# A new hand-written order for the first chunk of a fused attention and feed-forward kernel

## The chip, the cores and the metric

The kernel runs on one core of a Trainium2 chip. The metric is the device time of one execution in microseconds (us); lower is better. All times of the trace are counted from the first instruction of the profiled execution. PE stands for TensorE, DVE for VectorE, ACT for ScalarE, POOL for GpSimd, SP for SyncE.

## What is computed

Eight batches of eight heads with 576 positions and 64 features each go through masked attention. Heads 0 to 3 see the last 32 positions ("local"), heads 4 to 7 the positions with the same remainder modulo 32 ("strided"). The result, 4608 rows of 512, goes through two matrices with a softplus between them.

```
scores = where(mask, (q @ k.T) / 8, -1e9)            # 8 x 8 heads, 576 x 576
attn   = softmax(scores) @ v                         # 576 x 64 a head
x      = attn, heads side by side                    # 4608 x 512
h      = x @ w_in                                    # 512 -> 2048
g      = maximum(h, 0) + log1p(exp(-abs(h)))
out    = g @ w_out                                   # 2048 -> 512
```

## The kernel before, in words

Heads are worked in pairs: four pairs a batch, 32 in all (n = 0 to 31). The feed-forward part goes over nine chunks of 512 rows, and in each chunk over sixteen slices f of 128 hidden features. Each of x, g and the weights is split into a high and a low part, and three matmuls of 512 columns (high*high, twice, and low*high) stand for one product. So a chunk and slice takes 12 matmuls for `hidden` (L648, x to h) and 12 for `output` (L688, g to the result). The weights come as 64-bit floats and are turned into two 32-bit parts on the chip, once, in the first chunk; later chunks use the parts that lie in SBUF.

The first chunk therefore carries four kinds of work at once: the attention of pairs 0 to 3 (without which no feed-forward matmul can start), the attention of pairs 4 to 7, the conversion of 32 weight tiles, and the feed-forward of chunk 0 and the first two slices of chunk 1. Its order is written out by hand: `FIRST` (L36) is one string of task names, and at L946 a loop calls each task once, in this order. Every engine and every DMA queue works through its own instructions in the order in which the tasks issued them, waiting where a semaphore says so. From the third slice of chunk 1 on, a planner (`Plan`, with costs and due times) makes the order; the change does not touch it.

Three more lists, `ON_POOL`, `ON_VECTOR` and `ON_SCALAR`, say which engine does a task that several can do; a task in none of them goes to its usual engine.

The names: a letter or two, then the pair n or the slice f, and for pairs a part or half.

| name | what it does | engine (usual) |
|---|---|---|
| `q4`, `k4`, `v4` | DMA of pair 4's q, k, v, on SP's queue | SP (L261, L282, L293/L300) |
| `wi4`, `wo4` | DMA of slice 4's tile of w_in, w_out, 512 KB | SP (L569, L575) |
| `D4` (`D00`, `D01` a head) | q laid out for the score matmuls | ACT (L264) |
| `S40`, `S41` | score matmuls, part 0 and 1 | PE (L340, L355) |
| `X`, `x`, `E` | maximum of each row, its negative, exponentials | DVE (L389), DVE/POOL (L393), ACT (L399) |
| `Y`, `E`, `Z` | the same for the parts 00, 11, 20, 30 in wide form | DVE, ACT (L381), DVE (L385) |
| `r`, `R`, `M` | sum plus 1e-9, reciprocal, multiplication | DVE (L439), DVE, POOL or DVE (L447) |
| `T`, `C` (n < 4) | transposes by matmul and their copies out of PSUM | PE, ACT or DVE (L264) |
| `P` (n > 3) | 16 transposes on VectorE | DVE (L457) |
| `V40`, `V41` | weighted sums with v, by halves | PE (L525) |
| `H`, `L` | high and low part of x out of PSUM | ACT (L563), DVE (L561) |
| `ai`, `Bi`, `di`, `ci` (`ao`...) | four steps of the conversion of a w_in (w_out) tile | ACT (L589), DVE (L593, L602, L619) |
| `hi`, `li` (`ho`, `lo`) | high and low 32-bit part of the tile | ACT or POOL (L264), POOL or DVE (L634) |
| `F4`, `O4` | `hidden` and `output` of slice 4 (`Fa` the first three pairs of x alone) | PE (L648, L688) |
| `A`, `Ae`, `Al`, `u` | abs, exp, log, then the softplus sum | ACT three times, DVE (L669) |
| `Gh`, `Gl` | high and low part of g | ACT or DVE or POOL, POOL or DVE (L681) |
| `Qa`, `Q`, ... | the same steps for slices 0 and 1 of chunk 1 | |
| `y0` to `y3` | results of chunk 0 to DRAM | ACT or DVE, then SP (L704) |

Buffers that order work: one PSUM bank for scores of pairs 4 and up (`ps`), one for the sums with v (`pv`), two for `hidden` (`ph`), two buffers for u, three each for the parts of g, four for the conversion. K of pair n lies in one of two tiles, `kT`, so `k8` may be loaded when `S61` has read pair 6's. Pair 4's q lands where pair 3's probabilities were.

```
        for name in names:
            first[name]()
        plan.run()
```

Of the kernel before, what the change touches and what calls it, by code (L numbers as in the profile page):

```python
# [33 lines left out]


FIRST = """  # L36
q0 D00 k0 W mask D01 S01 q1 X01 x01 D11 q2 D10 S00 X00 Y00 E01 D20 E00 Z00 r0 D21 R0 M0 k1 S10 X10
S11 wi2 ai2 X11 Y11 E11 T00 wi4 k2 S20 ai4 Bi2 x10 E10 di2 k3 ci2 Bi4 Z11 hi2 di4 r1 ci4 T01 C01
C00 q3 D30 D31 T02 X20 R1 Y20 M1 v0 V00 C02 H00 wi1 E20 ai1 S21 X21 L00 Z20 T10 wi0 li2 x21 T11
hi4 Bi1 di1 ci1 E21 r2 V01 H01 L01 C11 wo0 S31 C10 R2 v1 hi1 S30 X30 wo14 li4 wo1 T12 Y30 ai0 X31  # L40
M2 V10 H10 L10 T21 k4 C12 Bi0 v2 wi3 x31 E30 di0 Z30 V11 C21 E31 H11 T20 C20 li1 L11 ao1 T22 r3 R3
M3 V20 T32 ao0 ci0 C22 Bo0 H20 L20 C32 hi0 ai3 T30 C30 do0 wo3 li0 T31 V21 v3 co0 C31 V31 H21 L21
ho0 V30 Bi3 di3 ao3 H30 Fa0 Bo3 ci3 hi3 H31 L30 wi10 q4 D4 L31 F0 lo0 A0 Fa1 do3 co3 li3 Ae0 ho3
Al0 Bo1 do1 u0 S40 X40 wo4 ao4 lo3 Bo4 wo2 ao2 x40 Bo2 Gh0 Gl0 wi8 ai8 wo9 wi6 Bi8 E40 F1 F3 A3
Ae3 do2 di8 ci8 hi8 Al3 co2 do4 co1 ho1 wo5 A1 Ae1 Al1 u3 li8 Gh3 O0 lo1 ho2 lo2 ai6 u1 wi5 ai5
S41 wi11 X41 x41 Gl3 Bi5 Gh1 Gl1 ai11 Bi11 Bi6 E41 F4 wo7 q5 D5 wi9 wi15 F2 A2 di5 O1 di11 Ae2 Al2
di6 ci5 r4 hi5 ci6 wi14 R4 wi12 ci11 hi11 k5 wi13 u2 Gh2 M4 S50 X50 F8 co4 x50 P4 Gl2 O2 li11 A4
Ae4 hi6 ho4 li5 li6 Al4 u4 E50 S51 X51 v4 V40 ai9 Bi9 di9 x51 A8 wo6 Ae8 Al8 wi7 k6 q6 lo4 wo11
ao5 Bo5 O3 ci9 ai7 Bi7 di7 u8 Gh4 Gl4 F5 H40 L40 E51 ci7 ai10 Bi10 r5 R5 F6 Gh8 do5 D6 S60 hi7
di10 Gl8 co5 M5 V41 ci10 A5 Ae5 Al5 u5 O4 li7 A6 Ae6 Al6 X60 x60 u6 ho5 P5 Gh5 Gl5 hi9 lo5 wo12  # L50
li9 F7 H41 hi10 ao7 li10 v5 O5 ao6 Bo6 do6 L41 co6 E60 S61 X61 Gh6 Gl6 A7 Ae7 Al7 x61 Bo7 k7 V50
u7 F9 ho6 lo6 O6 wo10 H50 L50 ai13 Bi13 wo8 ao8 E61 q7 V51 Bo8 D7 di13 do7 A9 Ae9 ci13 r6 R6 hi13
S70 do8 li13 F13 co8 H51 co7 M6 Al9 u9 Gh7 ao10 X70 x70 L51 ho8 Gl7 F10 P6 ho7 ai12 lo7 Gh9 Gl9
lo8 E70 Bi12 Bo10 O7 ao9 Bo9 do10 S71 v6 V60 do9 k9 O8 co9 ho9 A13 Ae13 Al13 u13 F11 di12 A10 Ae10
Al10 Gh13 X71 u10 ao11 Bo11 co10 ho10 lo9 lo10 Gh10 Gl10 x71 H60 L60 do11 ai14 Bi14 O9 A11 V61
ci12 di14 E71 r7 R7 O10 hi12 ai15 ci14 Ae11 li12 H61 L61 co11 hi14 M7 li14 wo15 Al11 u11 F12 P7
Gh11 Gl11 wo13 ao12 A12 Ae12 F14 ho11 lo11 Gl13 ao13 Al12 u12 Gh12 A14 Ae14 Bo12 do12 Gl12 co12
ho12 O11 Bi15 di15 lo12 ci15 ao15 Bo15 v7 V70 H70 L70 ao14 Bo14 Qa0 Al14 u14 O12 q8 D8 hi15 li15
Bo13 do13 co13 ho13 lo13 do14 co14 ho14 V71 H71 F15 A15 Ae15 L71 O13 Q0 Gh14 Gl14 lo14 O14 Al15
u15 Gh15 Gl15 Q1 v8 do15 co15 ho15 lo15 QA0 Qu0 QA1 O15 y0 Qh0 k8 Ob15 Ql0 y3 y2 Qu1 Qh1 Ql1 y1 q9  # L60
"""
# [958 lines left out]
```

## Time and profile before

| what | us |
|---|---|
| median of 3 runs (lowest 898.74, highest 899.64) | 899.62 |
| the profiled execution's own time | 898.62 |
| span of its instructions | 896.8 |
| PE busy | 878.9 |
| DVE busy | 601.3 |
| ACT busy | 446.8 |
| POOL busy | 58.1 |

The profile is one execution. Busy time is the time in which at least one instruction of the engine was running. A row of the timeline reads: start, duration, engine, line, operation, tile written<-tiles read, shapes, how many, and in brackets how long the engine sat idle before it and whose end released it. A row of the windows gives busy time and number of instructions of each engine in a stretch; a row of the waits gives total, number and longest. Matmuls overlap their successors, so their starts tell more than their durations.

### The profile page before, as it was taken

How to read it: one execution, taken by the hardware profiler on the slowest of the kernel's cores; microseconds unless marked ns; L12 is line 12 of the kernel's file. 1: busy time of each engine (PE TensorE's matmuls, PEld its weight loads, DVE VectorE, ACT ScalarE, POOL GpSimd, SP SyncE). 2: the span in 40 equal slices, each digit the busy share in tenths (PEclk: the TensorE clock that was granted, in tenths of full speed). 3: DMA queues.
4: the chain of work that ended last, by engine and by line, in shares of the span. 5: the costliest groups of instructions: out<-in, count | busy, mean ns of one | idle time of the engine just before them, and what ended most of it. 6: DMA issues, size and time to landing. Idle time of an engine off the chain costs nothing.

```text
span 896.8 us, 14347 instructions
## 1 busy us (share of the span) xinstructions
PE 878.9 (98%) x5632; PEld 722.0 (81%) x5632; DVE 601.3 (67%) x1313; ACT 446.8 (50%) x795; POOL 58.1 (6%) x81
## 2 busy tenths in 40 slices
PE   6899999999999999999999999999999999999998
PEld 4777777888888888888888888888888888888886
DVE  8999996877777677666766676776776333333332
ACT  7998765445444545544544444454443343333332
POOL 6244330000000000000000000000000000000000
PEclk9999999999999999999999999999999999999999
DMA  9882212112211112111211121111200010001001
...
DMA packets 50083, 58.27 MB, mean 65 GB/s; under 512 B 3168, under 2 KB 35296, under 8 KB 50016
## 3 DMA queue, kind: packets, MB, share of 16 engines
...
q8 instruction: 44, 0.72, 0.3%
q10 hardware_dynamic: 288, 0.33, 0.1%
...
## 4 chain that ended last, share of the span: by engine, by line
PE 87%; DVE 8%; ACT 2%; issue 1%; POOL 1%; DMA 0%; SPq 0%; DVEq 0%; POOLq 0%; ACTq 0%
PE py L688 41%; PE ph L648 40%; PE ps L355 2%; PE pv L525 2%; DVE pt L457 2%; PE po L525 1%; PE po L355 1%; DVE a_i L602 1%; DVE a_i L619 1%; DVE a_i L593 1%; DVE u L669 1%; DVE a_o L602 1%; DVE st L389 1%; DVE a_o L619 0%; DMA kT<-in_qk_dram 0%
## 5 line engine op out<-in xcount | busy, mean ns | idle before, releaser
L688 PE MATMUL py<-w_o,gh 128*128 128x512 f32 x1152 | 359.2, 393 | 0.3 <-POOL w_o L634 0.2
L648 PE MATMUL ph<-x_h,w_i 128*128 128x512 f32 x1152 | 356.4, 391 | 1.3 <-DVE w_i L634 0.9
L660 ACT ACTIVATE u<-ph 128x512 f32<-128x512 f32 x144 | 86.2, 599 | 396.8 <-PE ph L648 394.7
L648 PEld LDWEIGHTS ph<-x_h,w_i 128*128 128x128 f32 x1152 | 215.6, 188 | 47.2 <-DVE w_i L634 1.2
L688 PEld LDWEIGHTS py<-w_o,gh 128*128 128x128 f32 x1152 | 214.1, 188 | 47.7 <-POOL w_o L634 1.1
L648 PE MATMUL ph<-x_l,w_i 128*128 128x512 f32 x576 | 224.4, 390 | 0.0
L688 PE MATMUL py<-w_o,gl 128*128 128x512 f32 x576 | 224.4, 390 | 0.0
L669 DVE SCALAR_TENSOR_TENSOR u<-ph,u 128x512 f32<-128x512 f32 x144 | 99.2, 689 | 169.5 <-ACT u L665 167.9
L457 DVE STREAM_TRANSPOSE pt<-prob 32x192 f32<-32x192 f32 x448 | 137.1, 314 | 6.4
L688 PEld LDWEIGHTS py<-w_o,gl 128*128 128x128 f32 x576 | 108.2, 188 | 22.6
L648 PEld LDWEIGHTS ph<-x_l,w_i 128*128 128x128 f32 x576 | 108.2, 188 | 22.5
L681 DVE TENSOR_TENSOR gl<-u,gh 128x512 fp32r<-128x512 f32 x137 | 94.8, 692 | 12.0 <-POOL gh L264 0.8
L663 ACT ACTIVATE u<-u 128x512 f32<-128x512 f32 x144 | 91.2, 633 | 4.5
L665 ACT ACTIVATE u<-u 128x512 f32<-128x512 f32 x144 | 91.0, 632 | 4.3
L264 ACT COPY qT<-prob 64x576 f32<-64x576 f32 x56 | 70.6, 1261 | 2.3 <-DMA prob<-in_qk_dram 1.9
L264 DVE CAST gh<-u 128x512 fp32r<-128x512 f32 x130 | 55.7, 428 | 10.6 <-DVE u L669 0.5
L416 DVE TENSOR_TENSOR prob<-ps,mask_b 128x384 f32<-128x384 f32 x24 | 13.4, 558 | 50.2 <-PE ps L355 50.2
L355 PEld LDWEIGHTS ps<-kT,qT 128*64 128x64 f32 x720 | 24.0, 138 | 9.6 <-issue 8.1
L355 PE MATMUL ps<-kT,qT 128*64 128x64 f32 x720 | 27.6, 225 | 0.9 <-DMA kT<-in_qk_dram 0.9
L525 PE MATMUL pv<-pt,v_in 128*64 128x96 f32 x396 | 22.1, 248 | 1.0 <-PE ps L355 1.0
L447 DVE TENSOR_TENSOR prob<-prob,st 128x576 f32<-128x576 f32 x27 | 21.6, 799 | 0.9
L416 DVE TENSOR_TENSOR prob<-po,mask_b 128x192 f32<-128x192 f32 x24 | 8.6, 357 | 19.3 <-ACT x_h L563 19.3
(101 smaller groups left out, 511.9 us busy)
## 6 DMA issues: line engine op xcount, KB each, us to landing
...
```

Of the source, the lines that this page charges most:

```text
L264: (engine.copy if engine is nc.scalar else engine.tensor_copy)(dst, src)
L355: nc.tensor.matmul(ps[rows[place], 64 * (x - lo) : 64 * (x - lo) + 64], lhsT=blocks_of(n)[:, c // 32].rearrange("p h l -> p (h l)"), rhs=k ...
L416: nc.vector.tensor_tensor(pv, sv, m, op=ALU.add)
L457: nc.vector.transpose(pt[32 * (i + c) : 32 * (i + c) + 32, h, a : a + hi - lo, 32 * i : 32 * i + 32,], src[:, lo:hi, 32 * c : 32 * c + 32],)
L525: nc.tensor.matmul(po[64 * h : 64 * h + 64, TILE * x : TILE * x + TILE], lhsT=vs[n][:, a, h, :], rhs=pt_of(n, a)[:, h, a % 2], start=True, ...
L648: nc.tensor.matmul(ph, lhsT=w32["i", f][:, half, cc * P : (cc + 1) * P], rhs=x_of(x, cc)[:, t0 : t0 + n], start=(i == 0), stop=(i == 3 * N ...
L660: nc.scalar.activation(us[c, f], phs[c, f], AF.Abs)
L663: nc.scalar.activation(u, u, AF.Exp, scale=-1.0)
L665: nc.scalar.activation(u, u, AF.Ln, bias=1.0)
L669: nc.vector.scalar_tensor_tensor(u, in0=phs.pop((c, f)), scalar=0.0, in1=u, op0=ALU.max, op1=ALU.add)
L681: engine.tensor_tensor(g, us.pop((c, f)), ghs[c, f].bitcast(F32), op=ALU.subtract)
L688: nc.tensor.matmul(py[t], lhsT=g[:, sl], rhs=w32["o", f][:, half], start=(f == 0 and n == 0), stop=(f == NFC - 1 and n == 2),)
```

## The change

Only the tables change: the string `FIRST` holds the same names in another order, and the lists of engines hold other names. No function, no buffer and no planner cost changes. The first two lines of the order and the lists, in full:

```diff
 FIRST = """
-q0 D00 k0 W mask D01 S01 q1 X01 x01 D11 q2 D10 S00 X00 Y00 E01 D20 E00 Z00 r0 D21 R0 M0 k1 S10 X10
-S11 wi2 ai2 X11 Y11 E11 T00 wi4 k2 S20 ai4 Bi2 x10 E10 di2 k3 ci2 Bi4 Z11 hi2 di4 r1 ci4 T01 C01
...
+W mask q0 D00 k0 D01 S00 X00 Y00 q1 D11 S01 X01 E00 x01 Z00 k1 D10 S11 X11 q2 D20 Y11 E01 r0 wi0
+S10 X10 D21 x10 k2 S21 ai0 wo0 q3 D31 S20 R0 M0 E10 Bi0 di0 ci0 X21 hi0 E11 T00 x21 C00 ao0 Z11 r1
...
 ON_POOL = """
-x01 D10 D20 hi2 D30 hi0 hi3 ho1 x50 hi6 Gh8 x60 hi13 x70 ho9 Gh13 x71 ho11 hi15 ho14 Gh15 ho15
+D10 D20 x10 D31 hi0 x21 r2 x31 r3 hi3 hi1 ho1 Gh0 ho2 x41 hi4 r4 x50 x51 x60 Gh6 x61 r6 ho8 ho10
+ho9 x71 r7 hi14 hi15 ho13 ho14 ho15
 ON_VECTOR = """
-D00 M1 C21 M3 li0 lo0 li3 Gl0 li8 Gh3 lo1 Gl3 Gl1 lo4 Gl8 M5 Gl6 li13 lo9 lo10 Gl10 li12 M7 Gl12
-lo12 li15 lo13 Gh14 Gl14 lo14 Gl15 lo15
+D01 M0 C00 M3 li3 li1 li2 lo1 Gl0 li9 lo2 li4 Gl1 Gl4 li6 lo6 Gl6 lo7 Gl7 li12 lo8 M6 Gl9 lo11
+li14 M7 lo13 Gl14 Gl15
 ON_SCALAR = """
-y3
+y1 y3
```

The list for POOL has one line more, so every later line number is higher by one in the changed kernel. What this does to the instructions is shown at three places, as the built programs hold them.

VectorE, from the multiplication of pair 3 (`M3`) to the low part of pair 2's second half (`L21`). A name like `a_i_0` is the conversion buffer of w_in's tile 0, `a_o_0` of w_out's, `x_l1<-pv_2_0` the low part of x from pair 2, half 0. Before:

```order
L447 TENSOR_TENSOR prob_103<-prob_103,st_3_425 128x9x64
L619 SCALAR_TENSOR_TENSOR a_i_0_444<-ri_0_361,a_i_0_444 128x512
L593 TENSOR_SCALAR a_o_0_541<-a_o_0_541 128x512
L561 TENSOR_TENSOR x_l1_548<-pv_2_0_523,x_h1_546 128x288
L602 SCALAR_TENSOR_TENSOR a_o_0_541<-ro_0_395,a_o_0_541 128x512
L634 TENSOR_TENSOR w_i_0_551<-a_i_0_444,w_i_0_551 128x512
L619 SCALAR_TENSOR_TENSOR a_o_0_541<-ro_0_395,a_o_0_541 128x512
L561 TENSOR_TENSOR x_l1_548<-pv_2_1_582,x_h1_546 128x288
```

The same place on VectorE in the changed kernel:

```order
L448 TENSOR_TENSOR prob_103<-prob_103,st_3_353 128x9x64
L620 SCALAR_TENSOR_TENSOR a_i_1_386<-ri_1_368,a_i_1_386 128x512
L594 TENSOR_SCALAR a_i_2_512<-a_i_2_512 128x512
L562 TENSOR_TENSOR x_l1_525<-pv_2_0_515,x_h1_523 128x288
L603 SCALAR_TENSOR_TENSOR a_i_2_512<-ri_2_510,a_i_2_512 128x512
L635 TENSOR_TENSOR w_i_3_528<-a_i_3_396,w_i_3_528 128x512
L635 TENSOR_TENSOR w_i_1_576<-a_i_1_386,w_i_1_576 128x512
L562 TENSOR_TENSOR x_l1_525<-pv_2_1_579,x_h1_523 128x288
```

The tiles of slice 0 are converted earlier now, and tiles 1, 2 and 3 of w_in stand here instead.

ScalarE around the laying out of pair 6's q (`D6`, the two copies to `qT`), from the high parts of g's slice 4 and of pair 4's x on. `w_i_7<-a_i_7` is `hi7`, the activation from `ps_5_1` is `E51`. Before:

```order
L264 CAST gh_0_4_1016<-u_0_4_941 128x512
L563 CAST x_h0_331<-pv_4_0_970 128x288
L399 ACTIVATE prob_103,st_5_893<-ps_5_1_958,st_5_893 128x64 x3
L589 ACTIVATE a_i_10_1039<-ri_10_634 128x512
L264 COPY qT_99<-prob_103 64x18x32
L264 COPY qT_99<-prob_103 64x32x18
L264 CAST w_i_7_1077<-a_i_7_1011 128x512
L660 ACTIVATE u_0_5_1092<-ph_0_5_1020 128x512
```

The same place on ScalarE in the changed kernel:

```order
L564 CAST x_h0_325<-pv_4_0_971 128x288
L265 CAST gh_0_4_981<-u_0_4_936 128x512
L400 ACTIVATE prob_103,st_5_856<-ps_5_1_951,st_5_856 128x64 x3
L265 CAST w_i_7_1002<-a_i_7_849 128x512
L590 ACTIVATE a_o_4_1006<-ro_4_897 128x512
L265 COPY qT_99<-prob_103 64x18x32
L265 COPY qT_99<-prob_103 64x32x18
L661 ACTIVATE u_0_8_1024<-ph_0_8_989 128x512
```

`hi7` stood behind `D6` and stands ahead of it now, and `E51`, `D6` come after the first steps of slice 5 instead of before them.

SP's queue near the load of pair 8's k (`k8`, the DMA into `kT_0`). `prob` is a load of q (`q8` before, `q7` after). Before, with `v8` ahead and the results `y0` to `y2` (`out_0_dram`) around it:

```order
L261 DMA prob_103<-in_qk_dram 128x576
L293 DMA v_in_102<-in_v_dram 96x128
L300 DMA v_in_102<-in_v_dram 128x5x128
L704 DMA out_0_dram<-o_0_0_1778 128x512
L282 DMA kT_0_100<-in_qk_dram 128x576
L704 DMA out_0_dram<-o_0_3_1792 128x512
L704 DMA out_0_dram<-o_0_2_1795 128x512
```

SP's queue near the same load in the changed kernel, where `v5` stands ahead:

```order
L294 DMA v_in_102<-in_v_dram 96x128
L301 DMA v_in_102<-in_v_dram 128x5x128
L262 DMA prob_103<-in_qk_dram 128x576
L576 DMA ro_9_1228<-in_moe_w_out_dram 128x512
L283 DMA kT_1_101<-in_qk_dram 128x576
L283 DMA kT_0_100<-in_qk_dram 128x576
L570 DMA ri_13_1322<-in_moe_w_in_dram 128x4x128
```

`k8` left its place behind the first result and follows `k7` now.

On TensorE the score matmuls `S41`, `S50`, `S60` and `S70` each have one block of 12 feed-forward matmuls less ahead of them than before, and `S71` has three more.

More of the change, by code (lines that the diff above doesn't have):

```diff
@@ L36 @@
 FIRST = """
-q0 D00 k0 W mask D01 S01 q1 X01 x01 D11 q2 D10 S00 X00 Y00 E01 D20 E00 Z00 r0 D21 R0 M0 k1 S10 X10
-S11 wi2 ai2 X11 Y11 E11 T00 wi4 k2 S20 ai4 Bi2 x10 E10 di2 k3 ci2 Bi4 Z11 hi2 di4 r1 ci4 T01 C01
-C00 q3 D30 D31 T02 X20 R1 Y20 M1 v0 V00 C02 H00 wi1 E20 ai1 S21 X21 L00 Z20 T10 wi0 li2 x21 T11
-hi4 Bi1 di1 ci1 E21 r2 V01 H01 L01 C11 wo0 S31 C10 R2 v1 hi1 S30 X30 wo14 li4 wo1 T12 Y30 ai0 X31
-M2 V10 H10 L10 T21 k4 C12 Bi0 v2 wi3 x31 E30 di0 Z30 V11 C21 E31 H11 T20 C20 li1 L11 ao1 T22 r3 R3
@@ L42 @@
[L42 to L59, printed above, removed]
@@ L60 @@
-u15 Gh15 Gl15 Q1 v8 do15 co15 ho15 lo15 QA0 Qu0 QA1 O15 y0 Qh0 k8 Ob15 Ql0 y3 y2 Qu1 Qh1 Ql1 y1 q9
+W mask q0 D00 k0 D01 S00 X00 Y00 q1 D11 S01 X01 E00 x01 Z00 k1 D10 S11 X11 q2 D20 Y11 E01 r0 wi0
+S10 X10 D21 x10 k2 S21 ai0 wo0 q3 D31 S20 R0 M0 E10 Bi0 di0 ci0 X21 hi0 E11 T00 x21 C00 ao0 Z11 r1
+X20 T01 C01 Bo0 D30 v0 R1 do0 V00 H00 T02 C02 L00 Y20 co0 M1 k3 S31 X31 E21 E20 Z20 V01 li0 wi1
+S30 H01 L01 ai1 Bi1 r2 di1 x31 R2 M2 wi3 ai3 T10 C10 T11 C11 v1 T12 ho0 lo0 Bi3 V10 T21 X30 Y30
+di3 C12 H10 L10 V11 E30 T20 E31 Z30 C21 ci3 H11 v2 L11 r3 R3 M3 C20 ci1 T22 wi2 ai2 Bi2 V20 C22
@@ new lines @@
+H20 L20 di2 hi3 li3 T32 k4 wo1 C32 wi9 T31 ao1 T30 C31 v3 C30 hi1 li1 V21 H21 wo2 ao2 L21 V31 wi4
+V30 ci2 Bo1 Bo2 ai9 H31 L31 Fa0 q4 H30 L30 F0 wi10 do1 co1 Bi9 di9 wo3 Fa1 hi2 li2 D4 S40 ci9 A0
+Ae0 Al0 ho1 lo1 ao3 F1 u0 Gh0 X40 x40 F2 Bo3 Gl0 ai4 Bi4 hi9 li9 di4 do2 co2 ho2 v4 A1 ci4 E40 S41
+X41 x41 wi5 ai5 q5 Bi5 Ae1 Al1 u1 wo15 D5 lo2 O0 wi6 hi4 di5 li4 F3 Gh1 Gl1 O1 ci5 A2 Ae2 wi8 ai8
+do3 co3 ai10 k5 E41 S50 r4 hi5 wo12 Bi8 li5 Al2 A3 di8 u2 R4 Ae3 M4 Al3 wi7 ai7 ci8 wi12 hi8 X50
+x50 F4 u3 Gh3 Bi10 di10 ci10 F5 Gh2 Gl2 wo5 wo4 ho3 lo3 E50 P4 O2 A4 Gl3 q6 hi10 ao5 Bo5 Ae4 Al4
@@ new lines @@
+u4 wi11 S51 A5 Ae5 li8 X51 li10 ai6 Al5 Bi7 di7 V40 ci7 H40 x51 Gh4 Gl4 E51 r5 F8 hi7 do5 u5 ao4
+L40 O3 D6 Bi6 A8 Ae8 Al8 wi14 V41 H41 Bo4 li7 di6 do4 co4 ho4 ci6 hi6 R5 M5 k6 wo6 lo4 co5 Gh5 S60
+u8 Gh8 X60 F7 ao6 ho5 x60 E60 Gl5 li6 F6 A6 O4 ai11 L41 P5 wo7 ao7 wo8 Gl8 A7 Bo6 do6 Bo7 Ae6 Al6
+v5 V50 H50 S61 Ae7 Al7 lo5 O5 co6 ho6 u6 Gh6 Bi11 L50 do7 X61 x61 ai12 Bi12 F9 lo6 q7 wo9 D7 Gl6
+V51 co7 di12 E61 di11 ci11 H51 L51 ho7 k7 S70 X70 ci12 u7 lo7 hi11 li11 r6 k8 A9 O6 ao9 Bo9 x70
+Gh7 Ae9 Gl7 ao8 F11 do9 Bo8 do8 co8 Al9 u9 wi13 ai13 Bi13 di13 hi12 li12 wi15 ho8 lo8 co9 wo10
@@ new lines @@
+ao10 Bo10 O7 R6 ci13 M6 A11 do10 hi13 F10 O8 co10 ho10 Ae11 Al11 Gh9 u11 Gh11 ho9 lo9 F12 Gl9 O9
+lo10 P6 wo11 A10 Ae10 Al10 u10 ao11 Bo11 ao12 E70 S71 ai15 do11 Bi15 v6 V60 q8 Gl11 A12 Ae12 co11
+li13 F13 Gh10 H60 X71 L60 ai14 Bo12 V61 k9 Gl10 wo14 di15 H61 Al12 do12 L61 u12 Bi14 co12 O10 wo13
+ho11 lo11 di14 ci14 ci15 A13 Ae13 Al13 u13 Qa0 x71 E71 r7 hi14 R7 O11 li14 Gh13 F14 ho12 lo12 Gh12
+Gl12 O12 Gl13 A14 Ae14 Al14 M7 P7 u14 hi15 li15 ao13 Bo13 ao14 do13 co13 ao15 v7 V70 ho13 H70 F15
+A15 L70 V71 H71 lo13 Bo14 do14 co14 ho14 lo14 O13 Ae15 L71 v8 Al15 u15 Gh15 Q1 Gh14 Gl14 O14 Bo15
@@ L61 @@
+do15 D8 Q0 QA1 co15 Gl15 Qu1 QA0 Qu0 ho15 lo15 O15 Qh0 y0 Ob15 q9 y1 Qh1 Ql0 y2 y3 Ql1
 """
 ON_POOL = """
-x01 D10 D20 hi2 D30 hi0 hi3 ho1 x50 hi6 Gh8 x60 hi13 x70 ho9 Gh13 x71 ho11 hi15 ho14 Gh15 ho15
+D10 D20 x10 D31 hi0 x21 r2 x31 r3 hi3 hi1 ho1 Gh0 ho2 x41 hi4 r4 x50 x51 x60 Gh6 x61 r6 ho8 ho10
+ho9 x71 r7 hi14 hi15 ho13 ho14 ho15
 """.split()
 ON_VECTOR = """
-D00 M1 C21 M3 li0 lo0 li3 Gl0 li8 Gh3 lo1 Gl3 Gl1 lo4 Gl8 M5 Gl6 li13 lo9 lo10 Gl10 li12 M7 Gl12
-lo12 li15 lo13 Gh14 Gl14 lo14 Gl15 lo15
+D01 M0 C00 M3 li3 li1 li2 lo1 Gl0 li9 lo2 li4 Gl1 Gl4 li6 lo6 Gl6 lo7 Gl7 li12 lo8 M6 Gl9 lo11
```

## The prediction, made before the changed kernel was run

> **What bounds the kernel now.** I read the page first: the span and the busy rows of the engines.
>
> ```profile
> span 896.8 us, 14347 instructions
> PE 878.9 (98%) x5632; PEld 722.0 (81%) x5632; DVE 601.3 (67%) x1313; ACT 446.8 (50%) x795; POOL 58.1 (6%) x81
> ```
>
> TensorE is busy for 878.9 of 896.8 us, so it sat idle for 17.9 us in all. The change neither adds nor removes a matmul; it can win or lose only in that idle time. Where the idle time lies is told by the windows: the attention before the first feed-forward matmul, the rest of the first chunk, the seam to the planner's part, and a stretch behind it.
>
> ```profile
> 0.00:33.00 33.00, 22.40 (x482) 17.34 (x483) 28.60 (x61) 25.85 (x69) 18.40 (x42) 1.00 0.88 306
> 33.00:143.00 110.00, 107.47 (x666) 84.99 (x665) 104.84 (x222) 88.14 (x201) 39.67 (x39) 1.00 0.42 144
> 143.00:150.00 7.00, 6.06 (x57) 4.81 (x57) 4.14 (x8) 3.35 (x6) 0.00 (x0) 1.00 0.83 276
> 300.00:400.00 100.00, 100.00 (x640) 82.86 (x639) 71.30 (x164) 47.79 (x73) 0.00 (x0) 1.00 0.17 50
> ```
>
> The first figure behind the comma is PE, then its weight loads, DVE, ACT, POOL, the clock, the DMA share. TensorE idles for 10.6 us up to 33, for 2.5 us from 33 to 143, for 0.94 us at the seam, and not at all from 300 to 400, where the planner's order is untouched. VectorE is the second full engine: 104.84 of the 110 us of the first chunk. So both are near their limit there, and a kernel that idled nowhere after 33 us would be only 3.5 us shorter. The waits of TensorE between 33 and 150 us name the places:
>
> ```profile
> PE pv L525 <- PE ps L355: 1.0, 1, 1.0
> PE ps L355 <- DMA kT<-in_qk_dram: 0.9, 1, 0.9
> PE ph L648 <- DVE w_i L634: 0.9, 1, 0.9
> PE ph L648 <- DVE u L669: 0.3, 1, 0.3
> PE py L688 <- POOL w_o L634: 0.2, 1, 0.2
> ```
>
> Then I looked at how the feed-forward starts, in the timeline of TensorE, VectorE and ScalarE around 32 us:
>
> ```profile
> 32.00 0.72 PE L525 MATMUL pv<-early_l,room 128*64 128x96 f32 x12 [0.16 <-DVE x_l L561]
> 32.64 0.73 PE L648 MATMUL ph<-x_h,w_i 128*128 128x512 f32 x2
> 31.05 0.40 ACT L563 CAST x_h<-pv 128x288 fp32r<-128x288 f32 x1
> 31.50 0.45 DVE L561 TENSOR_TENSOR x_l<-pv,x_h 128x288 fp32r<-128x288 f32 x1
> 25.39 0.31 ACT L399 ACTIVATE prob<-py,st 128x64 f32<-128x64 f32 x1 [0.94 <-DVE st L393]
> ```
>
> The first feed-forward matmul, `Fa0`, begins at 32.64, behind `V30`, which waited for the one PSUM bank of the sums until `L21` had emptied it (31.50 to 31.95). `L21` began 0.05 us behind the end of `H21` on ScalarE (31.45). So VectorE and ScalarE reach this point together, and both must get earlier for `Fa0` to get earlier. The last row is the one long wait of ScalarE on that way: `E31` waited 0.94 us for `x31` on VectorE.
>
> **Part 1, the start.** The durations of the steps come from the rows by line (minimum, median and maximum in ns):
>
> ```profile
> L593 DVE TENSOR_SCALAR a_i<-a_i x16: 411/420/1512, 11.0 to 123.0; 128x512 uint32<-128x512 uint32 x16
> L602 DVE SCALAR_TENSOR_TENSOR a_i<-ri,a_i x16: 681/692/1784, 11.6 to 123.4; 128x512 uint32<-128x512 uint32 x16
> L619 DVE SCALAR_TENSOR_TENSOR a_i<-ri,a_i x16: 631/686/1783, 12.3 to 124.7; 128x512 uint32<-128x512 uint32 x16
> L634 DVE TENSOR_TENSOR w_i<-a_i,w_i x6: 673/686/1635, 30.3 to 127.0; 128x512 fp32r<-128x512 f32 x6
> L393 DVE TENSOR_SCALAR st<-st x7: 152/163/1270, 11.5 to 84.0; 128x3 f32<-128x3 f32 x5, 128x6 f32<-128x6 f32 x2
> L439 DVE TENSOR_SCALAR st<-st x32: 157/172/1240, 9.3 to 686.8; 128x9 f32<-128x9 f32 x32
> L589 ACT ACTIVATE a_i<-ri 128x512 f32<-128x512 f32 x16 | 10.7, 675 | 0.0
> ```
>
> Ahead of `L21` VectorE loses `x10`, `x21`, `x31` (0.49), `r2`, `r3` (0.34), `Bi4`, `di4`, `ci4` and `ci2` (0.42+0.69+0.69+0.69 = 2.49) and `li0` (0.69), 4.01 us together; it gains `x01` (0.16), `Bi3`, `di3`, `ci3` (1.80), `li1` and `li3` (1.37), 3.33 together. `M0` for `M1`, `C00` for `C21` and `D01` for `D00` are even. Net: 0.68 us less. Between `H10` and `H21` ScalarE has one `ai` or `ao` less, 2 instead of 3: 0.67 us less.
>
> The larger item is the maxima in these rows. They lie where GpSimd works at the same time:
>
> ```profile
> 18.88 1.28 POOL L634 TENSOR_TENSOR w_i<-a_i,w_i 128x512 fp32r<-128x512 f32 x1 [1.65 <-ACT w_i L264]
> 18.94 1.51 DVE L593 TENSOR_SCALAR a_i<-a_i 128x512 uint32<-128x512 uint32 x1
> 24.05 1.23 DVE L593 TENSOR_SCALAR a_i<-a_i 128x512 uint32<-128x512 uint32 x1
> ```
>
> `Bi1` began 0.06 us behind `li4` and ended 0.29 us behind its end, 1.09 us longer than usual; `Bi0` lost 0.81 and `r1` (the 1240 of L439) 1.07. That is 3.0 us ahead of `L21`. The new order may take back none of it or all of it, since GpSimd has about as many long steps there (`D10`, `D20`, `D31`, `M1`, `li0`, `M2`, `lo0` for `D10`, `D20`, `M0`, `D30`, `li2`, `li4`, `M2`, `li1`). I take half: 1.5. So VectorE alone would bring `L21` 0.7+1.5 = 2.2 us forward. ScalarE brings `H21` forward by its 0.67 and by the 0.94 of `E31`, because `x31` now stands on GpSimd, free of `Bi0`: 1.6. The later of the two sets the start, so `Fa0` comes 1.6 us earlier. Bounds: 2.5 earlier (ScalarE's shorter waits go too), and 0.5 later (the port costs what it did, and `x21`, `x31` wait on GpSimd behind `hi0`, `M1` and `li0`).
>
> **Part 2, the rest of the chunk.** VectorE has 3.8 us less to do over the whole chunk: one low part (0.69), four `x`, five `r`, `y1`, and two `Gh` go to the other engines; `Gh` and `y1` cost what these rows show.
>
> ```profile
> L264 DVE CAST gh<-u x130: 415/427/740, 46.0 to 887.6; 128x512 fp32r<-128x512 f32 x130
> L264 DVE COPY o<-py x17: 425/684/692, 144.0 to 893.0; 128x512 f32<-128x512 f32 x16, 128x256 f32<-128x256 f32 x1
> ```
>  With this less to do, the waits of `V50`, `F13`, `F8` and `O11` for VectorE and GpSimd go: 2.4 us of the five rows. What comes instead is waiting for ScalarE. `S41`, `S50`, `S60` and `S70` have one block of feed-forward matmuls less ahead of them, and they need laid-out q and the exponentials of the part before, out of one bank. The rows of ScalarE for `D6`, the cast behind it (`hi7`), `D7`, and of TensorE for `S60` and `S70`:
>
> ```profile
> 65.68 2.52 ACT L264 COPY qT<-prob 64x576 f32<-64x576 f32 x2
> 69.13 0.62 ACT L264 CAST w_i<-a_i 128x512 fp32r<-128x512 f32 x1 [0.93 <-DVE a_i L619]
> 86.20 2.56 ACT L264 COPY qT<-prob 64x576 f32<-64x576 f32 x2
> 70.77 0.35 PE L340 MATMUL ps<-mask_b,ident_b 128*64 128x384 bf16 x2
> 89.59 0.33 PE L340 MATMUL ps<-mask_b,ident_b 128*64 128x384 bf16 x2
> 156.06 2.72 PE ph L648 x12
> ```
>
> `D6` ended at 68.20, 2.57 us before `S60`; `D7` at 88.76, 0.83 us before `S70`. One block is 2.72 us (last row). So this slack is used up: of the 2.57 at `S60` nothing is left, and `S70` would wait 1.9 if ScalarE were as late as now. ScalarE's list from `D6` to the last input of `S70` is one cast (0.62, the row of `hi7`) shorter, and its waits there should be fewer, so I put 0.7 at `S70` (with `O6` and `F11` queued behind it), 0.3 each at `S60` and `S41`, 0.7 for `F4` and `F8`, which take over a bank as soon as `u2` and `u4` are done (`u4` stands behind the transposes of pair 4), and 0.6 for the last forty us: 2.6 against the 2.4 that go. Net 0.2 us lost. Bounds: 1.5 gained (a third of the list comes true) and 3 lost.
>
> **Part 3, the seam.** SP's queue shows why `S8` waited 0.94 us for its k:
>
> ```profile
> 142.50 0.35 SPq L704 DMA_DIRECT2D out_dram<-o  x1
> 142.91 0.42 SPq L282 DMA_DIRECT2D kT<-in_qk_dram  x1
> 142.59 0.62 PE L648 MATMUL ph<-x_h,w_i 128*128 128x512 f32 x2
> 146.41 0.92 PE L355 MATMUL ps<-kT,qT 128*64 128x64 f32 x24 [0.94 <-DMA kT<-in_qk_dram]
> ```
>
> `k8` stood behind `y0`, the first result, and was issued at 142.91. After the change it stands behind `k7` and needs only `S61`, dozens of blocks earlier. The 0.94 go whole. `q9` stays behind `y0`; `S9` comes blocks later, and no wait of it stands among the five rows. What is late next at the seam is nothing that a row shows: `S8` stands behind a whole block of `hidden`.
>
> The other queues: `v5` and `q7` hold SP's queue until `V41` and `P5` are done, with `wo9`, `k7`, `k8`, `wi13`, `wi15`, `wo10`, `wo11` behind them; the first that is used is `k7`, for `S70`, and `S70` needs `D7` from the same `q7` anyway. I put nothing; if the cover is gone, the wait shows at `S70`, where 0.7 is put already.
>
> **The sum.** -1.6 + 0.2 - 0.94 = -2.3 us. The profiled execution took 898.62, its span and 1.8 around it, and is 1.0 below the median of the runs, 899.62. Set against the median: **897.3 us**. About 0.2% (1.8 us) is what a measurement of this kernel can tell from no change; the forecast lies just beyond it.
>
> **The rivals.**
>
> *The port gives it back (no change, 898.8).* The shared stalls of VectorE and GpSimd come again at other places. For it: GpSimd has as many long steps as before and two more short ones; a single collision costs 1.1 us (1783 against 686 in the rows), and the order rests on durations that need to hold for 140 us. Against it: 3 us of such stalls lie ahead of `Fa0` in before, and the steps that stalled there now stand elsewhere. Then part 1 keeps its 0.67, part 2 loses 0.8, part 3 stays: -0.8. [...]
>
> *ScalarE becomes the engine TensorE waits for (slower, 902.1).* Place: `D6` and `E61` in front of `S60` and `S70`. If the port stays as it was, `x`, `ci` and `u` reach ScalarE as late as now, and `hi7`, which waited 0.93 us for VectorE behind `D6`, now waits in front of it. Then part 1 is +0.5, `S70` waits its 1.9 instead of 0.7, `S60` and `S50` about 1 and 0.8, which makes part 2 +2.9, and with part 3 the sum is +2.5. It decides from `S70` beginning later than about 89.6, where it began before: then the 2.7 of the block that it was moved forward are lost whole, and less the 0.94 that is 1.8. Against it: ScalarE is busy for only 88 of 110 us.
>
> That the tables do nothing can be excluded: the rows of the built program differ on every engine.
>
> **How the numbers follow.** The forecast has a chance of 0.55, the port rival 0.33, the ScalarE rival 0.11, and 0.01 is left for the rest. The likeliest case alone reaches from 895 to 897.8. The low end of the range takes the good bounds of parts 1 and 2: -2.5 - 1.5 - 0.94 = -4.9, 894.7. The high end holds the port rival and leaves out most of the ScalarE rival: 900.4. Faster by over 0.2%: 0.55; within: 0.34; slower: 0.11.
>
> **What would show it.** Right: the first L648 near 31.0; VectorE's L593 and L439 without their maxima ahead of it; `S8` without the wait for kT; small new waits of L340 and L355 for ScalarE between 40 and 90 us; the block behind `O15` near 141.2 instead of 142.59. Wrong: the first L648 at 32 or later, or long waits of `S60` and `S70`. If the sum is right with other parts, the working is wrong all the same.

## The result and the profile after

| kernel | median (lowest to highest), us | executions |
|---|---|---|
| before | 899.63 (898.74 to 899.64) | 4 |
| changed | 892.87 (892.08 to 893.86) | 4 |

The ratio is 0.9928, with a 95% interval from 0.9911 to 0.9945: the changed kernel is faster, by 6.76 us in the medians, where 2.3 were forecast. The profiled execution took 892.85, against 898.62 before: 5.77 less. The page, first the span, then the busy rows:

```profile
span 891.1 us, 14360 instructions
PE 879.2 (99%) x5632; PEld 724.3 (81%) x5632; DVE 593.0 (67%) x1300; ACT 446.6 (50%) x796; POOL 67.5 (8%) x93
```

TensorE is busy for nearly the same time as before (879.2, before 878.9), and idle for 11.9 us in place of 17.9. The windows of the changed kernel say where:

```profile
0.00:33.00 33.00, 25.76 (x489) 20.82 (x490) 28.01 (x61) 26.64 (x70) 20.05 (x46) 1.00 0.89 305
33.00:143.00 110.00, 109.21 (x710) 87.85 (x709) 100.19 (x213) 90.19 (x206) 47.44 (x47) 1.00 0.46 159
143.00:150.00 7.00, 7.00 (x33) 5.78 (x32) 5.99 (x14) 4.62 (x6) 0.00 (x0) 1.00 0.15 44
```

From 33 to 143 us TensorE idles for 0.8 us (2.5 before), VectorE for 9.8 (5.2 before), and GpSimd works for 47.4 (39.7). Of the five waits of TensorE between 33 and 150 us one other is left:

```profile
PE ph L649 <- DVE u L670: 0.8, 1, 0.8
```

The start of the feed-forward, in the timeline of TensorE, VectorE and ScalarE:

```profile
30.38 0.72 PE L526 MATMUL pv<-early_l,room 128*64 128x96 f32 x12 [0.50 <-DVE x_l L562]
31.02 0.73 PE L649 MATMUL ph<-x_h,w_i 128*128 128x512 f32 x2
29.88 0.44 DVE L562 TENSOR_TENSOR x_l<-pv,x_h 128x288 fp32r<-128x288 f32 x1
29.43 0.40 ACT L564 CAST x_h<-pv 128x288 fp32r<-128x288 f32 x1
```

`Fa0` begins at 31.02 in place of 32.64. `L21` (29.88) again follows `H21` (ends at 29.83) at once. The seam, SP and TensorE:

```profile
77.23 0.90 SPq L283 DMA_DIRECT2D kT<-in_qk_dram  x2
137.81 0.62 PE L649 MATMUL ph<-x_h,w_i 128*128 128x512 f32 x2
140.62 0.92 PE L356 MATMUL ps<-kT,qT 128*64 128x64 f32 x24
```

`k7` and `k8` are issued at 77 us, and `S8` follows its block without a wait: 2.81 us from the block's start, 3.82 before (142.59 to 146.41). So the ledger of the two traces is: `Fa0` 1.62 us earlier, and from `Fa0` to `S8` 109.60 us in place of 113.77, 4.17 less, of which 1.0 is the seam. Together 5.8, the whole gain of the profiled pair. Behind `S8` nothing changed: from its start to the start of TensorE's last matmul both traces give 746.18 us.

### The profile page after: what moved, and what is told of

Read it like the earlier page. It is cut to its first block, busy times and chain, and to the rows that moved or that the text cites. A ratio compares the mean times of both kernels' runs of the same rounds, so it can differ in the third digit from the quotient of the medians.

```text
span 891.1 us, 14360 instructions
## 1 busy us (share of the span) xinstructions
PE 879.2 (99%) x5632; PEld 724.3 (81%) x5632; DVE 593.0 (67%) x1300; ACT 446.6 (50%) x796; POOL 67.5 (8%) x93
## 4 chain that ended last, share of the span: by engine, by line
PE 93%; DVE 2%; ACT 1%; DMA 1%; SPq 1%; issue 0%; DVEq 0%
PE py L689 44%; PE ph L649 42%; PE ps L356 3%; PE pv L526 2%; PE po L526 1%; PE po L356 1%; DMA early_l<-in_qk_dram 1%; DMA ri<-in_moe_w_in_dram 1%; DVE a_i L603 0%; DVE w_i L635 0%; SPq L283 0%; ACT a_i L590 0%; DVE a_i L620 0%; ACT prob L400 0%; SPq L294 0%
## 5 line engine op out<-in xcount | busy, mean ns | idle before, releaser
L649 PE MATMUL ph<-x_h,w_i 128*128 128x512 f32 x1152 | 355.7, 390 | 0.8 <-DVE u L670 0.8
L649 PEld LDWEIGHTS ph<-x_h,w_i 128*128 128x128 f32 x1152 | 215.6, 188 | 46.3 <-DVE u L670 1.0
L649 PE MATMUL ph<-x_l,w_i 128*128 128x512 f32 x576 | 224.1, 389 | 0.0
L649 PEld LDWEIGHTS ph<-x_l,w_i 128*128 128x128 f32 x576 | 108.1, 188 | 22.5
L356 PEld LDWEIGHTS ps<-kT,qT 128*64 128x64 f32 x720 | 24.0, 137 | 8.5 <-issue 8.5
L356 PE MATMUL ps<-kT,qT 128*64 128x64 f32 x720 | 27.6, 225 | 0.0
```

What stands on the lines that cost most here:

```text
L356: nc.tensor.matmul(ps[rows[place], 64 * (x - lo) : 64 * (x - lo) + 64], lhsT=blocks_of(n)[:, c // 32].rearrange("p h l -> p (h l)"), rhs=k ...
L649: nc.tensor.matmul(ph, lhsT=w32["i", f][:, half, cc * P : (cc + 1) * P], rhs=x_of(x, cc)[:, t0 : t0 + n], start=(i == 0), stop=(i == 3 * N ...
```

## The experiments

All were timed beside the kernel before on one chip for a group of four; its medians there were 899.34, 899.22, 899.66 and 899.02. Ratios are to that kernel, with 95% intervals.

**Do the parts add? Half an order, lists alone, order alone.** Two kernels join one table up to `F0` with the other behind it, with the matching lists. In the first, the conversion steps that are open at the joint keep the changed kernel's order.

```diff
 FIRST = """          # e3_new_head
-<the old order up to F0>
+<the new order up to F0>
 <the old order of the rest>
```

> The changed kernel's order and engines up to the first hidden task (F0), then the remaining tasks in the order and on the engines of before; the conversion steps of tiles that stand open at that point keep the changed kernel's order. By separate gains the start keeps its 1.6 us, the chunk keeps the waits of before, and so does the seam: 1.6 us faster than before, first feed-forward matmul near 31.0. Rival, VectorE's backlog sets the pace of the chunk and the early start only lengthens the waits: within 0.5 us of before. Second rival, the whole gain follows from the early start: 5 us or more.

> The order and engines of before up to F0, then the remaining tasks as in the changed kernel (k8 early with them). By separate gains: first feed-forward matmul near 32.6 as before, chunk and seam gain 3.2 and 1.1, so 4.3 us faster than before. Rival, the chunk gains only because its start leaves VectorE fewer steps: less than 2.5 us faster.

New head, old tail: 905.29, ratio 1.0064 [1.0052, 1.0077]. Old head, new tail: 902.89, ratio 1.0037 [1.0023, 1.0050]. Both slower than either whole. The new head with the old tail, in the timeline of TensorE:

```profile
36.35 0.35 PE L341 MATMUL ps<-mask_b,ident_b 128*64 128x384 bf16 x2
42.59 1.54 PE L356 MATMUL ps<-kT,qT 128*64 128x64 f32 x24 [5.89 <-ACT qT L265]
```

ScalarE's waits from 30 to 45 us there:

```profile
ACT a_i L590 <- DVE w_i L635: 3.6, 1, 3.6
ACT w_i L265 <- DVE a_i L620: 2.4, 1, 2.4
```

And the window in the middle of TensorE's wait, with the granted clock at 0.50:

```profile
40.00:42.00 2.00, 0.00 (x0) 0.00 (x0) 1.75 (x2) 1.99 (x3) 0.97 (x1) 0.50 1.08 409
```

The head arrived as in the changed kernel (first L649 at 31.33), and the gain was gone 11 us later: the conversion steps left open at the joint stood in an order in which ScalarE had to wait 3.6 and 2.4 us, `D4` stood behind them in its queue, and `S40` behind that. The new tail behind the old head also lost its time soon behind the joint: TensorE waited for `u`, and ahead of that ScalarE for a weight tile (timeline of both).

```profile
44.94 1.22 PE L649 MATMUL ph<-x_h,w_i 128*128 128x512 f32 x2 [4.23 <-DVE u L670]
39.14 0.68 ACT L590 ACTIVATE a_o<-ro 128x512 f32<-128x512 f32 x1 [2.10 <-DMA ro<-in_moe_w_out_dram]
```

So neither half fits the other kernel's other half. What each half would be worth with a joint of its own making, these two runs do not show, since each lost its time at the joint.

Then the two kinds of table by themselves:

```diff
-FIRST, ON_POOL, ON_VECTOR, ON_SCALAR of the changed kernel
+e12_lists_alone: FIRST of before, the changed kernel's three lists
+e15_order_alone: FIRST of the changed kernel, the three lists of before
```

> The order of the kernel before with the changed kernel's three lists that give steps to GpSimd, VectorE and ScalarE: 13 instructions fewer on VectorE, 12 more on GpSimd, nothing moved in the order. If the waits of TensorE in before went because VectorE has less to do, as the prediction had it: the waits of V50, F13, F8 and O11 go here too, about 3 us by starts, and the time falls towards 896. If it is the order that did it, and the lists belong to it: steps that GpSimd now does at half the speed come late where they stand, new waits of several us come up and it is slower than before.

> The changed kernel's order with the lists of the kernel before, so that VectorE has 13 instructions more to do and GpSimd 12 fewer; the counterpart of the lists alone, which cost 14 us. If the lists are the part that carries (VectorE with less to do) and the order only follows: most of the gain is lost and long waits for VectorE come, 5 us or more above the changed kernel. If the order carries and VectorE's relief was not needed: within 1.5 us of the changed kernel.

Lists alone: 913.87, ratio 1.0154 [1.0141, 1.0168]. Order alone: 936.56, ratio 1.0409 [1.0393, 1.0425]. TensorE's waits from 33 to 160 us with the lists alone, the two largest:

```profile
PE ph L649 <- DVE u L670: 3.6, 6, 0.9
PE py L689 <- DVE w_o L635: 2.9, 2, 1.5
```

And with the order alone:

```profile
PE ph L648 <- DVE u L669: 5.9, 4, 3.0
PE ps L340 <- ACT prob L399: 4.8, 1, 4.8
```

With less on VectorE but the old order, the waits for VectorE became more, not fewer. Neither table has a gain of its own; only together do they fit.

**The seam by itself.** `k8` moved in before, twice, and put back in the changed kernel:

```diff
-... P6 ... k7 V50 ... v6 V60 do9 k9 ... y0 Qh0 k8 Ob15 ...
+e1_k8_early:  ... k7 k8 V50 ... v6 V60 do9 k9 ... y0 Qh0 Ob15 ...
+e5_k8_mid:    ... k7 V50 ... v6 V60 do9 k8 k9 ... y0 Qh0 Ob15 ...
+e10_k5_k8_early: as e5_k8_mid, and ... q5 k5 D5 wi9 wi15 ... in place of ... wi12 ... k5 wi13 ...
+e2_k8_late (changed kernel): k8 behind y0 instead of at 78 us
```

> The kernel before with one move: the load of pair 8's k goes from behind the first result to behind the load of pair 7's k. Three separate gains add up (start 1.6, chunk 3.2, seam 1.1 by the two traces): then this alone takes 1.1 us off the kernel before (the wait of 0.94 and about 0.2 of restart), and the traces agree up to 142 us. Rival, the transfer is hidden or another wait takes its place: within 0.3 us of the kernel before.

> The changed kernel with the same move undone: pair 8's k is loaded behind the first result. By three separate gains it loses 1.1 us against the changed kernel (about 5.7 us faster than before by the medians) and S8 waits 0.9 us for kT. Rival, the seam is worth nothing: within 0.3 us of the changed kernel.

`e2_k8_late`: 894.11, ratio 0.9944 [0.9931, 0.9956], 1.24 us above the changed kernel, with the old row back (a wait for kT of 1.0). `e1_k8_early`: 902.19, ratio 1.0034 [1.0022, 1.0047], slower. SP's waits from 50 to 95 us:

```profile
SPq L282 <- PE ps L355: 8.4, 1, 8.4
```

ScalarE's from 75 to 95 us:

```profile
ACT a_o L589 <- DMA ro<-in_moe_w_out_dram: 3.7, 1, 3.7
```

TensorE's from 33 to 160 us:

```profile
PE ps L355 <- ACT qT L264: 2.0, 1, 2.0
```

And a window behind that wait:

```profile
96.00:98.00 2.00, 2.00 (x5) 1.55 (x6) 2.00 (x5) 2.00 (x5) 0.00 (x0) 0.50 0.00 0
```

In before `k8` had to wait 8.4 us there for `S61`, and `wo10`, `wo8` and `q7` behind it on SP came late; ScalarE waited 3.7 us for `wo8`, `D7` stood behind that, and `S70` waited 2.0. That is the price of a load that stands too early in an in-order queue. In the changed kernel `k8` waits for nothing where it stands.

> The kernel before with one row of its order moved: the load k8 stands ahead of k9, behind the load v6, instead of at the end of the chunk. In the trace of before the buffer of kT that it fills has been free since about 83 us there and nothing stands behind it for 10 us, so no load behind it is held up, other than in the earlier attempt, where k8 stood ahead of wo10 and held it 8.4 us. If the seam is a gain of its own: the 0.94 us wait of S8 goes, 1.10 us by the starts of TensorE's instructions, so 1.1 us faster than before (ratio 0.9988), no new wait elsewhere. Rival, that any move in this tightly packed order brings a wait of its own: no gain or slower.

> The kernel before with two loads moved: k8 ahead of k9 as in the earlier run, and k5 right behind q5, ahead of the loads wi9, wi15, wi14 and wi12, which are needed later. In the trace of before k5 landed 0.36 us ahead of S50, in the run with k8 alone 1.63 us behind its need, in an order that is the same up to there, and the times of before fall into two groups about 1 us apart (898.6 to 899.2 and 899.6 to 900.7). If the groups are executions in which k5 came in time and too late: no execution in the upper group is left, S50 does not wait, and with the 1.1 us of the seam the median falls to 897.6 to 897.9 (ratio 0.9984). If they have another cause: two groups stay, the median is 898.2 or above.

`e5_k8_mid`: 898.63, ratio 0.9993 [0.9984, 1.0002], not told apart from before. `S8` did not wait, but in the profiled execution `k5` landed 1.63 us too late for `S50`:

```profile
55.94 0.92 PE L355 MATMUL ps<-kT,qT 128*64 128x64 f32 x24 [1.63 <-DMA kT<-in_qk_dram]
```

In the trace of before it landed 0.36 us ahead of `S50`, in that of the changed kernel 5.9 us ahead. With `k5` earlier as well (`e10_k5_k8_early`): 898.15, ratio 0.9984 [0.9974, 0.9993], faster; from `Fa0` to `S8` 112.76 us in place of 113.77. So the seam is a gain of its own, of 1.0 us, provided that nothing is pushed late by it. The theory that the two groups of times come from `k5` was not borne out: here one of ten executions lay 1 us above the lowest, but eight of eleven did in the next kernel that has both loads (`e11_k5_k8_l41`).

**Waits of VectorE taken away one at a time, in before.**

```diff
-... v5 O5 ao6 Bo6 do6 L41 co6 ...
+... v5 O5 ao6 L41 Bo6 do6 co6 ...        # e11_k5_k8_l41, with k5 and k8; e6_three_waits, with k8
-ON_VECTOR ... Gl6 li13 lo9 ...  ON_POOL ... hi13 x70 ...
+ON_VECTOR ... Gl6 lo9 ...  ON_POOL ... hi13 li13 x70 ...      # e6_three_waits
```

> The kernel before with three rows moved: k8 ahead of k9 (the seam), the cast-away L41 on VectorE ahead of Bo6 (V50 waited 1.00 us for it, 1.19 by starts), and li13 given to GpSimd ahead of M6 instead of VectorE, where it took 1.64 us beside M6 (F13 waited 0.89 us for it, 1.16 by starts). If a wait of TensorE is worth what it costs by the starts and nothing is late next: 1.10 + 1.19 + about 1.1, so 3.2 us faster than before (ratio 0.9964), and these three rows are gone from TensorE's waits. Rival (what the prediction assumed: the waits that go are replaced by waits for ScalarE): V50 earlier brings S70 earlier by about 1 us against D7 and E61, which have 0.83 us of slack in before, and F13 later has nothing to win; then about 1.5 to 2 us.

> As the kernel with k5 and k8 moved, and L41 ahead of Bo6 on VectorE, so that V50 doesn't wait (1.19 us by starts in before). If waits add up and what is late next is less late: 0.8 to 1.2 us faster than with the two loads alone (896.7 to 897.0). If S70 is late next, as the prediction assumed (0.83 us of slack): 0.5 us or less.

`e6_three_waits`: 898.94, ratio 0.9998 [0.9989, 1.0006]. `e11_k5_k8_l41`: 899.13, ratio 0.9990 [0.9981, 0.9999], no faster than with the two loads alone; from `Fa0` to `S8` 112.91 us in place of 112.76. The largest wait of TensorE from 33 to 160 us in `e11_k5_k8_l41`:

```profile
PE ph L648 <- DVE w_i L634: 1.6, 1, 1.6
```

In `e6_three_waits`:

```profile
PE ph L648 <- POOL w_i L634: 1.2, 1, 1.2
```

And the step of GpSimd that it waited for there, `li13`:

```profile
90.63 1.59 POOL L634 TENSOR_TENSOR w_i<-a_i,w_i 128x512 fp32r<-128x512 f32 x1
```

The wait of `V50` went in both. In `e11_k5_k8_l41` `S70` came 0.9 us earlier, counted from `Fa0`, than with the two loads alone, and `F13` waited the longer for `li13`: 1.6 us in place of 0.9. Counted in the same way, VectorE began `li13` as late as before (57.8 us behind `Fa0`, with the two loads alone 57.6). On GpSimd `li13` came no earlier: it could not begin before 90.63, behind `hi13`, and took 1.59 us. (`e6_three_waits` also lost 0.7 us to `k5`, which it leaves where it was.) Here a wait that was taken away was worth nothing, because the next step of the same engine was as late as before.

**How much room does the new order leave?** Two instructions of ScalarE, then two of VectorE, issued three times in the changed kernel, with the same result.

```diff
-        copy_on(engine, w32[w, f][:, 0], part[w, f].bitcast(F32))          # hi7; ai12 likewise
+        for _ in range(3 if (w, f) == ("i", 7) else 1):
+            copy_on(engine, w32[w, f][:, 0], part[w, f].bitcast(F32))
```

> The changed kernel with two instructions of ScalarE issued three times each, with the same result: the cast hi7 ahead of D6, 0.52 us by each more, and the magnitude ai12 ahead of D7, 0.57 by each more. ScalarE then has 1.05 us more to do ahead of S60 and 1.15 ahead of S70. If the new order left it as little room as the trace shows (D6 ended 0.54 ahead of S60, E61 0.34 ahead of S70): S60 waits 0.5 and S70 0.8, with 0.2 each for the restart 1.0 to 2.0 us slower than the changed kernel, and the waits of L341 and L356 for ScalarE stand in the list. If ScalarE has room to spare, as the absent waits could also mean: within 0.4 us of the changed kernel.

> The changed kernel with two instructions of VectorE issued three times each, with the same result: the sign steps co4 and co7, about 1.2 us more work at 67 us and 1.2 more at 82 us. The counterpart of the two tripled instructions of ScalarE (1.05 and 1.15 us more, 3.5 us slower). If the new order leaves VectorE some room: less than 1 us slower. If VectorE is as tight as ScalarE: 1.5 to 3.5 us slower, with TensorE waiting for x_l, u or w_i of VectorE.

ScalarE: 896.37, ratio 0.9963 [0.9949, 0.9977], 3.5 us above the changed kernel (2.9 above its second measurement, 893.44, below), and 113.50 us from `Fa0` to `S8`. VectorE: 895.87, ratio 0.9959 [0.9946, 0.9973], 2.4 above the 893.44 of the same group, and 113.33 us from `Fa0` to `S8`, in place of 109.92 in the trace of the changed kernel beside it. TensorE's waits from 33 to 160 us with ScalarE's instructions tripled:

```profile
PE ph L651 <- DVE u L672: 1.0, 1, 1.0
PE ph L651 <- DVE w_i L637: 1.0, 1, 1.0
PE ps L341 <- ACT prob L400: 0.9, 1, 0.9
PE ps L356 <- ACT qT L265: 0.4, 1, 0.4
```

And with VectorE's:

```profile
PE ph L650 <- DVE u L671: 1.8, 2, 1.1
PE ph L650 <- DVE w_i L636: 0.5, 1, 0.5
```

So neither engine has room for a microsecond more. `S60` (L356) and `S70` (L341) waited 0.4 and 0.9 us for ScalarE, about the added 1.05 and 1.15 less the room that the trace of the changed kernel shows. The theory that VectorE has room left fell: 1.2 us more twice cost nearly as much.

**The one wait left.** `F8` waits 0.79 us for `u4`. VectorE, GpSimd and TensorE there, in the changed kernel:

```profile
58.88 1.39 DVE L594 TENSOR_SCALAR a_o<-a_o 128x512 uint32<-128x512 uint32 x1
60.19 0.68 DVE L670 SCALAR_TENSOR_TENSOR u<-ph,u 128x512 f32<-128x512 f32 x1
57.44 2.54 POOL L635 TENSOR_TENSOR w_i<-a_i,w_i 128x512 fp32r<-128x512 f32 x2
60.92 0.50 PE L649 MATMUL ph<-x_h,w_i 128*128 128x512 f32 x1 [0.79 <-DVE u L670]
```

`Bo5` (58.88) stood beside `li10` of GpSimd and ended 0.29 us behind it, after 1.39 us instead of 0.41. In before `Bi1` ended 0.29 us behind `li4` in the same way (1.51 us, begun 0.06 us behind its start). What held the two steps the rows do not show.

```diff
-... ao5 Bo5 Ae4 Al4 u4 wi11 ...
+e7_u4_first:              ... ao5 u4 Bo5 Ae4 Al4 wi11 ...
+e9_bo5_late, e14_bo5_again: ... ao5 Ae4 Al4 u4 Bo5 wi11 ...
```

> The changed kernel with two steps of VectorE swapped: u4 ahead of Bo5. In its trace Bo5 stood beside li10 of GpSimd and took 1.39 us instead of 0.43, u4 came behind it, and F8 waited for u4, 0.79 us (0.99 by starts), the one wait of TensorE between 33 and 150 us. If that wait is the price of the port and ScalarE keeps up: the wait goes, 0.9 to 1.0 us faster than the changed kernel (about 891.9, ratio to before 0.9917). If ScalarE is at its limit there (D6 ended 0.54 us ahead of S60): S60 takes the place of F8 and 0.3 to 0.5 us are gained.

> The changed kernel with one step of VectorE moved by one place: Bo5 behind u4 instead of ahead of it, and nothing else on any engine (in the earlier attempt u4 had been put ahead of the exponential and the logarithm that it needs, which then waited for it). F8's wait, 0.99 us by starts, then has no cause left but the end of Al4. If what bounds the middle of the chunk is this one step of VectorE: the row goes, 0.8 to 1.0 us faster than the changed kernel (892.0, ratio to before 0.992). If ScalarE is at its limit: S60 waits for D6 instead and 0.3 to 0.5 us are gained.

> The changed kernel with Bo5 behind u4 once more, beside the changed kernel itself. In its first trace no wait of TensorE was left between the first feed-forward matmul and S8, and that stretch was 0.60 us shorter: 0.6 us faster than the changed kernel in the same comparison if that is what it is worth, 0 if the 0.6 us of the medians was the scatter of the executions.

> The changed kernel as it is, to have more of its times beside the two kernels below on the same chip: 892 to 894 us.

`e7_u4_first` says nothing on the question: `u4` also went ahead of the exponential and the logarithm of its own slice, so the softplus of slice 4 in the first chunk is another function there, and ScalarE's next step waited 2.49 us for `u4` (895.76, ratio 0.9960 [0.9948, 0.9973]). `e9_bo5_late`: 892.27, ratio 0.9909 [0.9896, 0.9923]; once more as `e14_bo5_again`: 893.34, ratio 0.9931 [0.9918, 0.9943], with the changed kernel beside it (`e13_changed_again`) at 893.44, ratio 0.9932 [0.9919, 0.9944]. The window of the second:

```profile
33.00:143.00 110.00, 110.00 (x713) 88.23 (x712) 100.11 (x215) 90.65 (x206) 47.47 (x47) 1.00 0.46 160
```

TensorE has no wait left in the chunk, and from `Fa0` to `S8` both traces give 109.00 us, 0.6 and 0.9 less than the two traces of the changed kernel. The medians differ by 0.6 and 0.1 us; within their intervals the two kernels are not told apart.

## Why the prediction was wrong

**Part 1, the start: the number right, the working in part.** -1.6 was forecast, -1.62 measured. `E31` no longer waited for `x31`, as the working had it. That ScalarE sets the start does not come out of the traces. `L21` follows `H21`, but `H21` in its turn follows `M3` on VectorE, through TensorE's transposes. `M3` before and in the changed kernel:

```profile
27.66 0.76 DVE L447 TENSOR_TENSOR prob<-prob,st 128x576 f32<-128x576 f32 x1
25.94 0.85 DVE L448 TENSOR_TENSOR prob<-prob,st 128x576 f32<-128x576 f32 x1
```

`M3` ends 1.63 us earlier (26.79 for 28.42), and from there to `L21` it takes 3.1 us in both. VectorE sat idle for only 0.17 us between 20 us and `L21` in before and for 0.10 in the changed kernel, so it was VectorE's queue that set the start. For VectorE 2.2 had been forecast, and 1.6 came: the size that the working gave to ScalarE.

That the number is met so closely is in part luck, since this stretch scatters. In the seven traces with the old opening the first L648 stands at 32.5 to 32.7 four times and at 33.6 to 33.8 three times; with the new opening, in nine traces, at 31.0 to 31.4 seven times, at 29.65 and 32.40 once each. What goes with the two groups of the old opening can be seen at the score matmuls near 6 us, the same 24 of them in each: they take 0.87 us in all four early traces, and 1.49 in all three late ones. The profiled execution of before, and `e11_k5_k8_l41`:

```profile
5.87 0.87 PE L355 MATMUL py<-early_l,early_h 128*64 128x64 f32 x24
6.28 1.49 PE L355 MATMUL py<-early_l,early_h 128*64 128x64 f32 x24
```

With the new opening the same block takes 0.92 us five times and 1.55 four times, and the start does not follow it: the four lie between 31.02 and 31.42. The profiled execution of before had the quick form, that of the changed kernel the slow one. That may be why the medians lie 6.76 apart and the profiled pair 5.77, and why the times of before fall into two groups 1 us apart; for the timed executions it was not shown, since they have no trace.

**Part 3, the seam: right.** -0.94 was forecast; in before, with `k5` moved too, it measures 1.0 (`e10_k5_k8_early`), and put back it costs 1.24 (`e2_k8_late`). That the queue past which `k8` moves costs nothing held for the new order only: in the old one the same place cost the whole gain and more (`e1_k8_early`).

**Part 2, the chunk: wrong.** +0.2 was forecast, and it came out at -3.2 (4.17 less the seam). This carries the miss of 3.4 us in the profiled pair (-5.8 for -2.3), and even the good bound of this part, 1.5 gained, was passed. Two terms failed.

First, "2.4 us of the five rows". A row gives idle time, and from start to start these waits cost more. Against the same matmuls without a wait, and with the second matmul behind a wait counted, which was late too, `V50` and `F13` lost 1.16 us each, `O11` 0.50 and `F8` 0.38, where the rows read 1.00, 0.89, 0.22 and 0.30. At two more places 0.06 us of idle time stood for 0.34. That is 3.9 us in place of 2.4.

Second, and larger, "`S70` would wait 1.9 if ScalarE were as late as now", from which 0.7 was taken for `S70`, 0.3 each for `S60` and `S41` and 0.6 for the last forty us. Of these 2.6 us only the 0.7 of `F4` and `F8` came, as 0.79 at `F8`, 0.85 from start to start. So 3.9 went and 0.85 came, which is 3.0 of the 3.2 us; the rest is spread over the stretch. ScalarE and TensorE in the changed kernel, `D6` and `S60`, `D7`, the end of `E61`, and `S70`:

```profile
64.06 2.54 ACT L265 COPY qT<-prob 64x576 f32<-64x576 f32 x2
67.13 0.33 PE L341 MATMUL ps<-mask_b,ident_b 128*64 128x384 bf16 x2
79.88 2.55 ACT L265 COPY qT<-prob 64x576 f32<-64x576 f32 x2
83.23 0.21 ACT L400 ACTIVATION_READ_ACCUMULATOR prob<-ps,st 128x1 f32 x1
83.78 0.33 PE L341 MATMUL ps<-mask_b,ident_b 128*64 128x384 bf16 x2
```

At `S60` the forecast was close: of the 2.57 us of slack 0.53 are left (67.13 less 66.60). At `S70` it was not. The last step of ScalarE that `S70` needs is `D7` before and `E61` in the changed kernel. From the start of `D6` to its end ScalarE took 19.38 us in place of 23.08, and `E61` ends 0.34 us ahead of `S70`. The window of that stretch in the kernel before (for ScalarE alone):

```profile
65.68:88.76 23.08, 19.93 (x45) 1.00 0.32 103
```

In the changed kernel:

```profile
64.06:83.44 19.38, 18.93 (x44) 1.00 0.65 225
```

ScalarE's waits in it, before:

```profile
ACT u L660 <- DVE gl L681: 1.1, 1, 1.1
ACT w_i L264 <- DVE a_i L619: 0.9, 1, 0.9
ACT a_o L589 <- POOL w_o L634: 0.8, 1, 0.8
```

And in the changed kernel:

```profile
ACT prob L400 <- POOL st L394: 0.3, 1, 0.3
```

ScalarE did 1.0 us less there and sat idle for 2.7 less. The prediction had counted one cast (0.62) and put the waits down as "fewer", 0.6 in effect, so 1.2 us where 3.7 came. That is the step: the waits of ScalarE for VectorE and GpSimd were read at one row (`hi7`), and not summed over the stretch, so the engine that was feared to become the bound had itself been held up by the others for most of what was feared. This is read from the two traces; no run takes these waits away by themselves. That the room is as small as feared, a few tenths, `e8_scalar_tripled` shows: a microsecond more on ScalarE brings the forecast waits of `S60` and `S70` about as large as forecast.

The reason given for the waits that go, that VectorE has 3.8 us less to do, is not enough: with the same lists and the old order the kernel became 14 us slower (`e12_lists_alone`), and a wait taken from VectorE in the old order came back at its next step (`e11_k5_k8_l41`). The new order without the lists was 38 us slower (`e15_order_alone`). So it takes order and lists together; which of the moved steps carry most is not settled.

The port rival ("no change") fell. Stalls of a microsecond are still there (`Bo5`, 1.39 us in place of 0.41), but between 33 and 143 us only this one reaches TensorE. That a port stands behind such stalls was the author's assumption: the rows show steps of VectorE that took longer beside steps of GpSimd, and not the cause. Work moved between the two engines by the lists alone cost 14 us, and by the lists together with their order it came with a gain of 6.76; whether such stalls made the lists alone slow was not shown. The ScalarE rival fell by the 0.34 us of room at `S70`.
